# A long convolution with a gated MLP, forward and backward: two kinds of tile turned by transposing DMAs instead of TensorE

## The chip, the cores and the metric

The program runs on one core of one Trainium2 chip. The metric is device time in microseconds (us). The kernel before took 745.42 us, the median of three runs from 744.89 to 746.04. A core has TensorE (PE, with its weight loads PEld), VectorE (DVE), ScalarE (ACT), GpSimd (POOL) and SyncE (SP). SP computes nothing here: it only issues DMAs, in the order of the program, and waits on semaphores in between. ACT and POOL issue some DMAs too.

## The reference

One input `x` of 2048 x 512 in bfloat16 is normalised over its rows and goes two ways; their product is added to `x`. All gradients but that of the unused input are wanted beside the output.

```python
def _A_ref(u, ...):                      # per channel d: a kernel of length L=2048, N=128 states
    P = exp((dt * A)[:, :, None] * l)    # A, B, C complex, 512 x 128
    K = einsum("dn,dnl,dn->dl", C, P, dt * B).real
    y = irfft(rfft(pad(u.T)) * rfft(pad(K)))[:, :L].T      # long convolution
    return y + u * Dskip
def _B_ref(x, w1, w2):                   # w1: 512 x 1792, w2: 1792 x 512
    return einsum("bsf,fd->bsd", silu(einsum("bsd,df->bsf", x, w1)), w2)
...
xn = _layernorm(x)
out = x + _A_ref(xn, ...) * silu(_B_ref(xn, w1, w2))
...
_out, _vjp = jax.vjp(f, u, A_re, A_im, B_re, B_im, C_re, C_im, log_dt, Dskip, w1, w2)
return (_out, *_vjp(grad_out))
```

## The kernel before, in words

Six stages follow one another; the engines overlap across their borders. The order on every engine is the order in which the code writes the instructions (a manual schedule). A tile has a fixed number of buffers; an instruction that takes a buffer again waits for its last reader. `later` puts a call on a list and `settle` carries the list out, so that a copy out of PSUM or a store is written behind other work; a call put on the list twice over (`later` of a `later`) comes one settle later.

Stage 1 (`stage_1`) does three things beside one another, in steps that Python counts as ticks:

- The forward MLP (`gen_ffn_fwd`). The 2048 rows go in four groups `tc_` of 512, the 1792 hidden columns in seven pairs of 128-column blocks (`f0` = 0, 2, ... 12): 28 steps. A step computes `ps_h` (L607, 8 products, two PSUM buffers); ACT reads it twice, as `aT` = silu (L609) and as `hs` (L610, four buffers, shared with `o2` of the second product); SP stores `hs` to DRAM as `hTd` (L611). The second product `ps_o` (L580) of the group before goes on in the same step, and its results are stored as `gd` and `od`.
- In each step `trans` (L556 to L564) turns the `aT` pair of the step before, 128 x 1024: eight PE transposes against an identity matrix into PSUM (`pt_a`, L561), a DVE copy into `ak` (two buffers), and SP's store to `akd` in DRAM, for a later stage's gradient of `w2`.
- The tables of the Fourier transform (`dft_table_phases`). Sixteen tables `tf` of 128 x 1024 are made by DVE and ACT (or mirrored by PE, `tb_m`); four buffers. In `C(t)` (L412) SP stores one to `TFd`, eight PE transposes (L417) turn it into PSUM, and `EV` copies it to `tb_i` (two buffers), in turn by DVE (L83) and by ACT (L85). `S(t)`, one tick later, stores `tb_i` to `TId` (L423). They come in 16 of the steps from the eighth on.
- The powers of the state matrix (`power_phases`), mostly DVE and ACT, stored to `XYd` (L510), two stores at a time. Stage 2 loads `TFd` and `XYd` again.

A step ends with one settle; in the step f0 = 10 of the first three groups there is one settle more inside it.

The stages 2 to 5 form the spectra, the convolution and its gradients, the gradient of `w2` and those of the state parameters. Stage 6 (`stage_6`) has 28 steps `B.dh(n)`: SP loads `hsb` from `hTd`, three steps ahead; ACT forms `sd` (L132); PE computes `ps_da` (L1870); DVE multiplies both into `dhT` (L1871); SP stores `dhd`. Seven transposing DMAs, issued by SP after the first seven steps, bring `W1T` from DRAM (L1950), which `ps_dx` (L1893) reads, beginning after the eighth `dh`. Sixteen further transposing DMAs load `dhc` for `ps_w` (L1981), the gradient of `w1`, in 16 groups of 16 products; ACT copies each to `o10b` (three buffers), SP stores it. Between these the first output is put together (`Out0`): eight pairs of 128-row tiles, the first four by POOL's queue (`pool=True`), the last four by ACT's (`q`, L1365): a store, and three loads of the tile pair two further on.

```python
q = k.nc.gpsimd if pool else k.nc.scalar
q.dma_start(k.o0_v[:, t0:t0 + TS, :], S[:])
self.load(t0 + 2 * TS, q)
```

Of the kernel before, what the change touches and what calls it, by code (L numbers as in the profile page):

```python
# [11 lines left out]
BF16 = mybir.dt.bfloat16  # L12
I32 = mybir.dt.int32
AX = mybir.AxisListType
P = 128
# [51 lines left out]
def later(k, fn, *a, **kw):  # L67

    k.after.append((fn, a, kw))
# [303 lines left out]
def dft_table_phases(k, pool):  # L373

    nc = k.nc
    kv = pool.tile([P, 512], I32, name="kv", tag="tb_r")
    nc.gpsimd.iota(kv[:], pattern=[[4, 512]], base=1, channel_multiplier=0)
    kf = pool.tile([P, 512], F32, name="kf")
    nc.vector.tensor_copy(out=kf[:], in_=kv[:])
    lf = pool.tile([P, T], F32, name="lf")  # L380
    nc.vector.tensor_scalar(out=lf[:], in0=k.lvf[:], scalar1=1.0 / 8192.0, scalar2=None, op0=ALU.mult)
    nJ = pool.tile([P, P], BF16, name="nJ")
    nc.gpsimd.memset(nJ[:], 0.0)
    nc.gpsimd.affine_select(out=nJ[:], in_=nJ[:], compare_op=ALU.not_equal, fill=-1.0, base=1 - P, pattern=[[1, P]], channel_multiplier=1)
    st = {}

    def A(t):
        r = pool.tile([P, 512], I32, name="tb_r", tag="tb_r")
        v = pool.tile([P, 512], F32, name="tb_v", tag="tb_v", bufs=2)
        frac(nc, v[:], r[:], kf[:], lf[:, t:t + 1])  # L390
        st[t] = v

    def B(t):
        v = st[t]
        w = pool.tile([P, 512], F32, name="tb_w", tag="tb_w", bufs=2)
        nc.scalar.activation(out=w[:], in_=v[:], func=ACT.Abs)
        tf = pool.tile([P, 4, 2, P], BF16, name="tb_f", tag="tb_f", bufs=4)
        rr = lambda ap: ap.rearrange("p (a b) -> p a b", b=P)
        nc.scalar.activation(out=tf[:, :, 1, :], in_=rr(v[:]), func=ACT.Sin, scale=-2.0 * math.pi)
        nc.scalar.activation(out=tf[:, :, 0, :], in_=rr(w[:]), func=ACT.Sin, scale=-2.0 * math.pi, bias=k.halfpi[:])  # L400
        st[t] = tf

    def M(t):

        tf, tm = st[t], pool.tile([P, 4, 2, P], BF16, name="tb_m", tag="tb_f", bufs=4)
        ps = k.pd.tile([P, 2, 4, P], F32, name="ps_m", tag="pd")
        for c in range(2):
            nc.tensor.matmul(out=ps[:, c], lhsT=nJ[:], rhs=tf[:, :, 1 - c, :], start=True, stop=True)
        later(k, nc.scalar.copy, out=tm[:].rearrange("p a c b -> p c a b"), in_=ps[:])
        st[16 - t] = tm  # L410

    def C(t):  # L412
        tf = st[t]
        nc.sync.dma_start(k.TFd[:, :, t].rearrange("a p c b -> p a c b"), tf[:])
        pt = k.ps.tile([P, 8, P], BF16, name="pt_ti", tag="pz", bufs=1)
        for i in range(8):
            nc.tensor.transpose(out=pt[:, i, :], in_=tf[:, i // 2, i % 2, :], identity=k.ident[:])  # L417
        ti = pool.tile([P, 8, P], BF16, name="tb_i", tag="tb_i", bufs=2)
        later(k, EV, k, ti[:], pt[:])
        st[t] = ti  # L420

    def S(t):
        nc.sync.dma_start(k.TId[:, t], st.pop(t)[:])  # L423
    return A, B, M, C, S


# [115 lines left out]
def gen_ffn_fwd(k, fs, W1, W2):  # L542

    nc = k.nc

    def xnt(tc_):
        XNT = fs.tile([P, DK, 4, P], BF16, name="XNT", tag="XNT")
        for h in range(2):
            pt = k.ps.tile([P, 2, 4, P], BF16, name="pt_x", tag="ps")
            for d_ in range(2):  # L550
                for t in range(4):
                    dk = 2 * h + d_
                    nc.tensor.transpose(out=pt[:, d_, t, :], in_=k.xn[:, 4 * tc_ + t, dk * P:(dk + 1) * P], identity=k.ident[:])
            (nc.scalar.copy if h else nc.vector.tensor_copy)(out=XNT[:, 2 * h:2 * h + 2], in_=pt[:])
        return XNT

    def trans(tc_, aT, f0):
        pt = k.ps.tile([P, 2, 4, P], BF16, name="pt_a", tag="ps")
        for j in range(2):
            for t in range(4):  # L560
                nc.tensor.transpose(out=pt[:, j, t, :], in_=aT[:, f0 + j, t * P:(t + 1) * P], identity=k.ident[:])  # L561
        ak = fs.tile([P, 2, 4, P], BF16, name="ak", tag="ak")
        later(k, nc.vector.tensor_copy, out=ak[:], in_=pt[:])
        later(k, nc.sync.dma_start, k.akd[f0:f0 + 2, :, 4 * tc_:4 * tc_ + 4].rearrange("f p t q -> p f t q"), ak[:])  # L564

    def gen_o(tc_, aT):
        for th in range(2):
            ts_ = slice(4 * tc_ + 2 * th, 4 * tc_ + 2 * th + 2)
            g2 = fs.tile([P, 2, D], BF16, name="g2", tag="g2")
            o2 = fs.tile([P, 2, D], BF16, name="o2", tag="hs", bufs=4)  # L570
            if tc_ == 3:
                G2 = G4[:, 2 * th:2 * th + 2]
            else:
                G2 = fs.tile([P, 2, D], BF16, name="G2", tag="G2", bufs=1)[:]
                nc.sync.dma_start(G2, k.g_v[:, ts_, :])
            for t in range(2):
                tt = 2 * th + t
                pso = k.ps.tile([P, D], F32, name="ps_o", tag="ps")
                for ft in range(FT):
                    nc.tensor.matmul(out=pso[:], lhsT=aT[:, ft, tt * P:(tt + 1) * P], rhs=W2[:, ft, :], start=(ft == 0), stop=(ft == FT - 1))  # L580
                    if ft == FT // 2 - 1:
                        yield
                later(k, nc.scalar.activation, out=g2[:, t, :], in_=pso[:], func=ACT.Silu)
                later(k, nc.scalar.copy, out=o2[:, t, :], in_=pso[:])
                if t == 0:
                    yield
            later(k, nc.sync.dma_start, k.tl(k.gd[:])[:, ts_, :], g2[:])
            later(k, nc.sync.dma_start, k.tl(k.od[:])[:, ts_, :], o2[:])
            later(k, later, k, nc.vector.tensor_tensor, out=k.DS[:, ts_, :], in0=G2, in1=g2[:], op=ALU.mult)
            yield  # L590

    prev = iter(())
    XNT = xnt(0)
    late = G4 = None
    for tc_ in range(4):
        if tc_ == 3:
            G4 = fs.tile([P, 4, D], BF16, name="G4", tag="XNT")
            nc.sync.dma_start(G4[:], k.g_v[:, 12:16, :])
        aT = fs.tile([P, FT, 512], BF16, name="aT", tag="aT")
        nxt = None  # L600
        for f0 in range(0, FT, 2):
            yield
            ps = k.pd.tile([P, 2, 512], F32, name="ps_h", tag="pd")
            for j in range(2):
                ft = f0 + j
                for dk in range(DK):
                    nc.tensor.matmul(out=ps[:, j], lhsT=W1[:, dk, ft * P:(ft + 1) * P], rhs=XNT[:, dk], start=(dk == 0), stop=(dk == DK - 1))  # L607
            hs = fs.tile([P, 2, 512], BF16, name="hs", tag="hs", bufs=4)
            nc.scalar.activation(out=aT[:, f0:f0 + 2, :], in_=ps[:], func=ACT.Silu)  # L609
            nc.scalar.copy(out=hs[:], in_=ps[:])  # L610
            nc.sync.dma_start(k.hTd[tc_][:, f0:f0 + 2], hs[:])  # L611
            next(prev, None)
            if f0 == FT - 2:
                next(prev, None)
            k.mid()
            if late:
                trans(*late)
            late = (tc_, aT, f0)
            if f0 == FT - 4 and tc_ < 3:
                settle(k)  # L620
                nxt = xnt(tc_ + 1)
        XNT = nxt
        prev = gen_o(tc_, aT)
    yield
    trans(*late)
    k.last_aT = aT
    for _ in prev:
        k.mid()
        yield
# [714 lines left out]
class Out0:  # L1344
# [15 lines left out]
    def run(self, t0, pool=False):  # L1360
        k, (S, g, x) = self.k, self.ins.pop(t0)
        TT = k.nc.vector.tensor_tensor
        TT(out=S[:], in0=S[:], in1=g[:], op=ALU.mult)
        TT(out=S[:], in0=S[:], in1=x[:], op=ALU.add)
        q = k.nc.gpsimd if pool else k.nc.scalar  # L1365
        q.dma_start(k.o0_v[:, t0:t0 + TS, :], S[:])
        self.load(t0 + 2 * TS, q)

# [555 lines left out]
def stage_6(k):  # L1924
    nc = k.nc
    lo, ro = k.left, k.right
    fw = k.fw
    W1T = k.tfp.tile([P, FT, D], BF16, name="W1T", tag="W1")
# [17 lines left out]
        nc.sync.dma_start_transpose(ch[i][:, 4 * tc_:4 * tc_ + 4, :], k.dhd[tc_, FC * i:FC * i + FC])  # L1946
    for n in range(28):
        B.dh(n)
        if n < 7:
            nc.sync.dma_start_transpose(W1T[:, 2 * n:2 * n + 2], k.ins["w1"][:, 256 * n:256 * n + 256])  # L1950
        next(prev, None)
        if n == 8 or n >= 21:
            next(fin, None)
# [19 lines left out]
    for i in range(4):  # L1973
        for dk in range(DK):
# [4 lines left out]
            ps = k.ps.tile([P, FC], F32, name="ps_w1", tag="ps")  # L1979
# [49 lines left out]
```

## Time and profile before

| | |
|---|---|
| median of three runs | 745.42 us (744.89 to 746.04) |
| the profiled execution, whole | 748.97 us |
| its span, first to last instruction | 747.2 us |
| PE busy | 659.1 us, 88% |
| DVE busy | 619.4 us, 83% |
| ACT busy | 418.1 us, 56% |
| POOL busy | 122.4 us, 16% |
| DMA | 198.83 MB, mean 266 GB/s |
| mean granted TensorE clock | 0.957 of full |

The profile is of one execution; its durations belong to that one. In a line of the groups view stand: the line of the kernel, the engine, the operation, what it writes and reads, its shape, how often it ran, busy us and mean ns, and the idle time of the engine just before, with what ended it. In the waits view: who waited, for whom, us in total, how often, the longest. In the view of one tile or line: how often an instruction ran, its duration in ns as smallest, median and largest, the start of the first and the last. In the timeline: start and duration in us. "SPq" is SP's queue; its durations are those of issuing a DMA, not of the transfer. "To landing" is the time from a DMA's issue to the landing of its data. In the windows view each engine's busy us stand for a stretch of the span, then the granted clock, the mean busy share of the core's 16 DMA engines, and their GB/s. That share counts packets whose times overlap and can pass 1.

### The profile page before, as it was taken

To read this page: it belongs to the slowest core of one execution; us is meant where nothing else is said; L and a number is where in the kernel's file an instruction comes from. 1 tells how busy PE (TensorE), PEld (TensorE's weight loads), DVE (VectorE), ACT (ScalarE), POOL (GpSimd) and SP (SyncE) were. 2 spreads that over 40 slices of the span, in tenths; PEclk is the share of its full clock that TensorE was granted. 3 is DMA by queue.
4 is the path that set the end of the run, shared out by engine and by line. 5 is a ranking of instruction groups with operands and counts; after the bars stand their busy time and mean duration, and the time that the engine had idled before them with its cause. 6 is when DMAs were issued, how large, how long until landed. Compare 5 with 4: busy or idle time off the path is not lost. (4 is left out here: it accounts for less than half of the span.)

```text
span 747.2 us, 13309 instructions
## 1 busy us (share of the span) xinstructions
PE 659.1 (88%) x5132; PEld 336.8 (45%) x5132; DVE 619.4 (83%) x965; ACT 418.1 (56%) x513; POOL 122.4 (16%) x184
## 2 busy tenths in 40 slices
PE   4778877799878777999999899999999979999988
PEld 2434444354545656554444344444444434444543
DVE  6799999989899799599999999944577549899570
ACT  4789888995568967365534322344656523443231
POOL 2334171021011002100001212041222002200000
PEclk9998998899999998999999999999999989999999
DMA  9647767889898978999767879799886997999992
GB/s 268 236 165 246 236 229 240 266 298 358 268 317 275 301 222 182 296 347 359 287 227 286 287 288 353 215 316 335 272 283 232 240 307 248 321 242 221 225 266 87
DMA packets 167361, 198.83 MB, mean 266 GB/s; under 512 B 58461, under 2 KB 128484, under 8 KB 161378
## 3 DMA queue, kind: packets, MB, share of 16 engines
q1 hardware_dynamic: 150882, 132.63, 58.1%
q0 software_dynamic: 11200, 51.98, 19.8%
q10 hardware_dynamic: 5216, 13.38, 5.4%
q8 instruction: 40, 0.66, 0.4%
q14 instruction: 23, 0.19, 0.1%
HBM read 105.38 MB, written 83.38 MB: 253 GB/s over the span
## 5 line engine op out<-in xcount | busy, mean ns | idle before, releaser
L607 PE MATMUL ps_h<-XNT,W 128*128 128x512 bf16 x224 | 60.8, 421 | 12.2 <-ACT hs L610 12.2
L1188 PEld LDWEIGHTS <-TIs 128*128 128x128 bf16 x384 | 37.7, 99 | 51.7 <-issue 4.9
L1893 PE MATMUL ps_dx<-W1T,dhT 128*128 128x512 bf16 x224 | 53.8, 384 | 5.5 <-DMA W1T<-in_B_w_dram 4.6
L580 PE MATMUL ps_o<-W,aT 128*128 128x512 bf16 x224 | 55.7, 399 | 2.5 <-DVE ak L76 2.5
L1870 PE MATMUL ps_da<-DOT,W2T 128*128 128x512 bf16 x224 | 53.9, 388 | 2.3 <-DVE dhT L1871 2.3
L1981 PE MATMUL ps_w<-dhc,xn 128*128 128x448 bf16 x256 | 51.3, 361 | 3.1 <-ACT o10b L1983 3.1
L1595 PE MATMUL ps_w<-DO_all,AW 128*128 128x512 bf16 x224 | 52.0, 380 | 0.0
L1871 DVE TENSOR_TENSOR dhT<-ps_da,sd 128x1024 bf16<-128x1024 f32 x28 | 34.1, 1222 | 18.9 <-ACT sd L132 14.0
L1902 ACT ACTIVATE dxn<-dxn,c,rstd 128x512 f32<-128x512 f32 x16 | 13.0, 814 | 65.6 <-DVE c L1901 65.6
L1781 DVE TENSOR_TENSOR T<-Vb,YTl 128x2048 bf16<-128x2048 bf16 x16 | 19.6, 1224 | 35.2 <-ACT Vb L1772 34.9
L1164 PEld LDWEIGHTS <-TFs 128*128 128x128 bf16 x312 | 30.1, 98 | 38.6 <-issue 2.1
L934 ACT COPY XT<-pt_xt 128x1024 bf16<-128x1024 bf16 (+1 forms) x44 | 41.4, 1009 | 5.2 <-DMA XTd<-XT 3.2
L1772 ACT CAST Vb<-ps_V 128x1024 bf16<-128x1024 f32 x32 | 31.7, 1013 | 16.8 <-PE ps_V L1770 11.5
L1164 PE MATMUL ps_f<-K_b,TFs 128*128 128x512 bf16 x168 | 39.1, 379 | 1.5 <-DMA K_b<-Kud 1.3
L607 PEld LDWEIGHTS <-W 128*128 128x128 bf16 x224 | 22.8, 106 | 38.3 <-issue 21.8
L1981 PEld LDWEIGHTS <-xn 128*128 128x128 bf16 x256 | 25.5, 100 | 28.1 <-issue 5.6
L580 PEld LDWEIGHTS <-aT 128*128 128x128 bf16 x224 | 22.9, 102 | 32.0 <-issue 8.3
L1893 PEld LDWEIGHTS <-dhT 128*128 128x128 bf16 x224 | 22.0, 99 | 33.3 <-issue 7.5
L1870 PEld LDWEIGHTS <-W2T 128*128 128x128 bf16 x224 | 22.0, 99 | 30.2 <-issue 6.4
L998 PE MATMUL ps_f<-xn,TFs 128*128 128x512 bf16 x128 | 32.7, 411 | 3.3 <-DMA TFs<-TFd 3.3
L1164 PE MATMUL ps_f<-DS,TFs 128*128 128x512 bf16 x144 | 33.0, 379 | 1.8 <-ACT S_s L1443 1.8
L932 PE MATMUL pt_xt<-ident_bfloat,X 128*128 128x128 bf16 x328 | 25.7, 228 | 8.9 <-ACT XT L934 6.9
(342 smaller groups left out, 1510.6 us busy)
## 6 DMA issues: line engine op xcount, KB each, us to landing
TIs<-TId SPq DMA_DIRECT2D x24, 512.0 KB, 6.6
XTd<-XT SPq DMA_DIRECT2D x20, 512.0 KB, 5.8
XTl<-XTd SPq DMA_DIRECT2D x15, 512.0 KB, 8.6
hTd<-hs SPq DMA_DIRECT2D x28, 256.0 KB, 3.5
akd<-ak SPq DMA_DIRECT2D x28, 256.0 KB, 3.3
UXl<-UXd POOLq DMA_DIRECT2D x7, 1024.0 KB, 7.7
dhd<-dhT SPq DMA_DIRECT2D x28, 256.0 KB, 4.2
XYd<-XYg SPq DMA_DIRECT2D x25, 256.0 KB, 4.0
```

The costliest lines, as they stand in the source:

```text
L580: nc.tensor.matmul(out=pso[:], lhsT=aT[:, ft, tt * P:(tt + 1) * P], rhs=W2[:, ft, :], start=(ft == 0), stop=(ft == FT - 1))
L607: nc.tensor.matmul(out=ps[:, j], lhsT=W1[:, dk, ft * P:(ft + 1) * P], rhs=XNT[:, dk], start=(dk == 0), stop=(dk == DK - 1))
L934: nc.scalar.copy(out=XT[:, j0:j0 + len(ks)], in_=pt[:, 0:len(ks)])
L998: nc.tensor.matmul(out=ps[:, c, :], lhsT=TFs[:, t1 + 4 * j, c, :], rhs=src[:, t1 + 4 * j, :], start=(j == 0), stop=(j == 3))
L1164: nc.tensor.matmul(out=ps[:, c, :], lhsT=tab(j), rhs=at(t1 + 4 * j), start=(n == 0), stop=(n == 4 * len(terms) - 1))
L1188: nc.tensor.matmul(out=ps[:, j, :], lhsT=TIs[:, j, 2 * kt + c, :], rhs=B[kt][:, c, (t0 + j) % 4, :], start=(kt == 0 and c == 0), stop=(kt ...
L1595: nc.tensor.matmul(out=ps[:], lhsT=A[:, t, :], rhs=k.DO[:, t, :], start=(t == 0), stop=(t == T - 1))
L1772: nc.scalar.copy(out=self.V[i][:, g2], in_=ps[:].rearrange("p b c n -> p c b n"))
L1870: nc.tensor.matmul(out=ps[:, j], lhsT=self.W2T[:, ft // 2, dk, j * P:(j + 1) * P], rhs=self.DOT[tc_][:, dk], start=(dk == 0), stop=(dk == ...
L1871: nc.vector.tensor_tensor(out=self.dhT[:, f0:f0 + 2, :], in0=ps[:], in1=sd[:], op=ALU.mult)
L1893: nc.tensor.matmul(out=psx[:], lhsT=dhT[:, ft, t % 4 * P:(t % 4 + 1) * P], rhs=self.W1T[:, ft, :], start=(ft == 0), stop=(ft == FT - 1))
L1981: nc.tensor.matmul(out=ps[:], lhsT=k.xn[:, t, dk * P:(dk + 1) * P], rhs=ch[i][:, t, :], start=(t == 0), stop=(t == T - 1))
```

## The change

- `C(t)`: the eight PE transposes, their PSUM tile and the copy by DVE or ACT go. SP issues one transposing DMA from the table in SBUF to `tb_i` in SBUF. 16 times.
- `trans`: likewise, one transposing DMA from `aT` to `ak`; the store to `akd` is put off by one settle more, since it now waits for a DMA. 28 times.
- `W1T`: the seven transposing DMAs are issued after the first four steps of stage 6, two after each (one after the fourth), instead of one after each of the first seven.
- `Out0.run`: the last four tile pairs are stored, and their followers loaded, by SP's queue instead of ACT's.

```diff
     def C(t):
         tf = st[t]
         nc.sync.dma_start(k.TFd[:, :, t].rearrange("a p c b -> p a c b"), tf[:])
-        pt = k.ps.tile([P, 8, P], BF16, name="pt_ti", tag="pz", bufs=1)
-        for i in range(8):
-            nc.tensor.transpose(out=pt[:, i, :], in_=tf[:, i // 2, i % 2, :], identity=k.ident[:])
         ti = pool.tile([P, 8, P], BF16, name="tb_i", tag="tb_i", bufs=2)
-        later(k, EV, k, ti[:], pt[:])
+        nc.sync.dma_start_transpose(ti[:], tf[:].rearrange("p a c b -> p (a c b)"))
         st[t] = ti
...
     def trans(tc_, aT, f0):
-        pt = k.ps.tile([P, 2, 4, P], BF16, name="pt_a", tag="ps")
-        for j in range(2):
-            for t in range(4):
-                nc.tensor.transpose(out=pt[:, j, t, :], in_=aT[:, f0 + j, t * P:(t + 1) * P], identity=k.ident[:])
         ak = fs.tile([P, 2, 4, P], BF16, name="ak", tag="ak")
-        later(k, nc.vector.tensor_copy, out=ak[:], in_=pt[:])
-        later(k, nc.sync.dma_start, k.akd[f0:f0 + 2, :, 4 * tc_:4 * tc_ + 4].rearrange("f p t q -> p f t q"), ak[:])
+        nc.sync.dma_start_transpose(ak[:].rearrange("p j t q -> p (j t) q"), aT[:, f0:f0 + 2, :].rearrange("p j t -> p (j t)"))
+        later(k, later, k, nc.sync.dma_start, k.akd[f0:f0 + 2, :, 4 * tc_:4 * tc_ + 4].rearrange("f p t q -> p f t q"), ak[:])
...
-        q = k.nc.gpsimd if pool else k.nc.scalar
+        q = k.nc.gpsimd if pool else k.nc.sync
         q.dma_start(k.o0_v[:, t0:t0 + TS, :], S[:])
...
-        if n < 7:
-            nc.sync.dma_start_transpose(W1T[:, 2 * n:2 * n + 2], k.ins["w1"][:, 256 * n:256 * n + 256])
+        for m in range(2 * n, min(2 * n + 2, 7)):
+            nc.sync.dma_start_transpose(W1T[:, 2 * m:2 * m + 2], k.ins["w1"][:, 256 * m:256 * m + 256])
```

## The prediction

> **What bounds the kernel now.** I read the windows first, then the groups of lines, the waits of SP's queue, single tiles and the timeline. The chain of work that ended last cannot be followed back before 392 us, so the first stage, in which nearly all of the change lies, is read from its own windows. Its 28 steps store one `hTd` each, and I take 17 to 181 us as the stretch around them.
>
> ```profile
> core 0: us, PE busy (x) PEld busy (x) DVE busy (x) ACT busy (x) POOL busy (x), PEclk, DMA share, GB/s
> 17.00:181.00 164.00, 137.51 (x877) 72.35 (x876) 154.54 (x312) 139.28 (x175) 44.06 (x36) 0.91 0.73 251
> 45.00:166.00 121.00, 98.74 (x632) 52.18 (x631) 116.31 (x223) 108.32 (x136) 34.45 (x28) 0.89 0.74 249
> ```
>
> From 45 to 166 us DVE is busy 116.3 of 121 us (96%), ACT 90%, PE 82%, and the DMA engines 74%. DVE is the bound there, with ACT close behind. SP is not in this table. Its queue waits in the stretch like this (the longest and the shortest of 21 rows, which sum to 94.9 us), and its stores mark the steps:
>
> ```profile
> SPq L611 <- ACT hs L610: 58.8, 24, 5.9
> ...
> SPq L76 <- DMA akd<-ak: 0.2, 1, 0.2
> ...
> L611 SPq DMA_DIRECT2D hTd<-hs x28: 319/320/581, 17.9 to 166.2; - x28
> ...
> 44.71 0.32 SPq L611 DMA_DIRECT2D hTd<-hs  x1
> 97.86 0.32 SPq L611 DMA_DIRECT2D hTd<-hs  x1
> 108.56 0.32 SPq L611 DMA_DIRECT2D hTd<-hs  x1
> ```
>
> So SP waits 94.9 us, 58.8 of them for ACT's `hs`, and issues for about 164 - 94.9 = 69.1 us. SP is in order: one wait holds back everything behind it. That slack is what the change spends. The store at 44.71 is the eighth of the 28: the seven steps up to it take 3.8 us each, the twenty after it 121.5 / 20 = 6.1 us; the longest is 10.7 us, from 97.86 to 108.56.
>
> **The change, part by part.** First what leaves the compute engines:
>
> ```profile
> L76 DVE COPY ak<-pt_a 128x1024 bf16<-128x1024 bf16 x28 | 19.1, 683 | 3.7 <-DMA akd<-ak 3.4
> L83 DVE COPY tb_i<-pt_ti 128x1024 bf16<-128x1024 bf16 x8 | 5.4, 680 | 1.5 <-DMA XYd<-XYg 1.5
> L85 ACT COPY tb_i<-pt_ti 128x1024 bf16<-128x1024 bf16 x8 | 8.5, 1059 | 0.0
> L561 PE MATMUL pt_a<-ident_bfloat,aT 128*128 128x128 bf16 x224 | 17.6, 224 | 0.5 <-DVE ak L76 0.5
> L417 PE MATMUL pt_ti<-ident_bfloat,tb_f 128*128 128x128 bf16 x72 | 5.6, 222 | 0.9 <-DVE tb_i L83 0.9
> L417 PE MATMUL pt_ti<-ident_bfloat,tb_m 128*128 128x128 bf16 x56 | 4.3, 219 | 0.0
> ```
>
> DVE loses 19.1 + 5.4 = 24.5 us, ACT 8.5, PE 27.5. In the stretch that leaves DVE 154.5 - 24.5 = 130.0, ACT 139.3 - 8.5 = 130.8, PE 110. With DVE's present idle time (164 - 154.5 = 9.5) on top, the engines alone could do the stretch in about 140 us: 24 us less, the most that this can bring.
>
> In their place SP issues 28 transposes of `ak` and 16 of `tb_i`, each 128 x 1024 bf16, 256 KB, from SBUF to SBUF. No such transfer is in the trace. The nearest is W1T's, also 256 KB, but out of DRAM; then `dhc`'s, 448 KB:
>
> ```profile
> L1950 SPq DMA_TRANSPOSE W1T<-in_B_w_dram x7: 1363/1452/1600, 581.7 to 597.7; - x7
> DMA to landing us min/median/max: 4.7/5.2/5.8
> ...
> L1946 SPq DMA_TRANSPOSE dhc<-dhd x16: 1537/1930/3315, 662.8 to 713.1; - x16
> ```
>
> A transpose occupies SP for 1.45 us and lands 5.2 us after its issue. Stores of that size are quicker:
>
> ```profile
> akd<-ak SPq DMA_DIRECT2D x28, 256.0 KB, 3.3
> ...
> 69.25 0.32 SPq L611 DMA_DIRECT2D hTd<-hs  x1
> 70.46 0.44 SPq L414 DMA_DIRECT2D TFd<-tb_f  x1
> 71.01 0.51 SPq L76 DMA_DIRECT2D akd<-ak  x1
> 71.56 1.09 SPq L510 DMA_DIRECT2D XYd<-XYg  x2
> 72.75 0.66 SPq L423 DMA_DIRECT2D TId<-tb_i  x1
> ```
>
> SP's new account, in five terms:
> (a) Issues: 44 x 1.45 = 63.8 us. Ends: 44 x 0.32 = 14 (`hTd`'s store) and 44 x 3.3 = 146 (the longest `dhc`). I take W1T's median, same size and same kind.
> (b) The store `TId` now waits on SP for its own transpose to land. In program order the transposes of `tb_i` and `ak`, an `akd` store and sometimes two `XYd` stores stand before it: 1.45 + 1.45 + 0.45 = 3.35, or 4.4 with 1.09 more. It lands at 5.2, so SP stands still 0.8 to 1.85, say 1.3, 16 times: 21 us. What is queued behind is the next `hTd`, whose `hs` has four buffers: engines can run two to three steps ahead, no more. At a landing of 3.3 the term is nothing, at 5.8 about 30.
> (c) At the three early settles (step f0 = 10 of the first three groups), `akd` stands one store behind its own transpose: 5.2 - 1.45 - 0.4 = 3.35, three times: 10 us; 5 at a landing of 3.3, 12 at 5.8.
> (d) `ak` has two buffers, and a buffer is held from the transpose's issue to the landing of its store: 5.2 + 0.4 + 3.3 = 8.9 per two steps, 4.4 a step. The first seven steps take 3.8 us now; 0.6 us more in each is 4 us; nothing at a landing of 3.3, 7 at 5.8. Later steps have room.
> (e) SP cannot work ahead of ACT, so a step that DVE makes long leaves SP idle. In the one of 10.7 us SP would have 0.32 + 0.44 + 1.45 + 1.45 + 0.51 + 1.09 + 0.66 = 5.9 us to do: 4.8 idle, of which I let half be filled by what it is behind with: 2.4; ends 0 and 4.8.
> Sum: 69.1 + 63.8 + 21 + 10 + 4 + 2.4 = 170.3 us, 6.3 more than the 164 of the stretch. SP becomes the bound, just. DVE's 24.5 us turn into DVE waiting for buffers.
>
> The DMA engines say nearly the same. Transposes go in small packets; here are the 16 us from 700 to 716 with hardly anything else, and then the rate in W1T's stretch (584 to 600 us):
>
> ```profile
> DMA packets 12515, 3.67 MB, mean 229 GB/s; under 512 B 11747, under 2 KB 12515, under 8 KB 12515
> q1 hardware_dynamic: 12515, 3.67, 110.7%
> ...
> q1 hardware_dynamic: 8389, 4.60, 113.1%
> ```
>
> 1.107 x 16 us x 16 engines / 12515 = 22.6 ns a packet. Without its 768 larger packets of about 1 KB the window leaves 2.9 MB in 11,747 packets, 249 B each, so I count 256 B: 256 KB are 1,024 packets, 1.45 us of all 16 engines; 44 are 64 us. The stretch has 0.73 x 164 = 120 us now, so 184 us, and at the highest share that I find held (113%) 163 us: as long as the stretch. Other end: at a copy's price (251 GB/s at 0.73 is 344 GB/s, 0.76 us each) it is (120 + 33) / 1.13 = 136 us. I keep 1.45, the price of the same kind. [...]
>
> W1T's, two a step instead of one:
>
> ```profile
> 588.42 0.54 SPq L1856 DMA_DIRECT2D hsb<-hTd  x1
> 593.16 1.06 ACT L132 ACTIVATE sd<-hsb 128x1024 bf16<-128x1024 bf16 x1 [1.63 <-DMA hsb<-hTd]
> 597.67 1.45 SPq L1950 DMA_TRANSPOSE W1T<-in_B_w_dram  x1
> 603.28 1.01 PE L1893 MATMUL ps_dx<-W1T,dhT 128*128 128x512 bf16 x2 [3.44 <-DMA W1T<-in_B_w_dram]
> ```
>
> SP issues without a gap here, so its order decides. The seventh transpose moves from 597.7 to about 593.6 and lands near 599, and PE's 3.4 us wait at 603.3 goes. But the `hsb` loads between are pushed back by the transposes ahead of them, that of 588.4 to 592.6. ACT already waits for it, so `sd` slips from 593.2 to about 597 and PE's next `ps_da` with it to about 599; the remaining seven `ps_dx` then end near 603.5 instead of 604.3. Net -0.8 us; ends -3.4 (PE's whole wait) and +4.2 (the load's whole delay).
>
> Out0's last four tiles: ten issues (four stores, six loads) leave ACT for SP.
>
> ```profile
> 720.27 13.95 PE L1981 MATMUL ps_w<-dhc,xn 128*128 128x448 bf16 x64 [2.69 <-ACT o10b L1983]
> 734.30 9.25 PE L1981 MATMUL ps_w<-dhc,xn 128*128 128x448 bf16 x48
> ```
>
> From 720.3 us PE runs to the end without an idle moment over 0.2 us, so ACT's freed issues bring nothing. What could cost: an `o10b` store stands behind four issues of 0.4 us, 1.6 us later. `o10b` has three buffers and 16 products of `ps_w` take 3.03 us (48 in 9.25), so it is needed 9 us later: 0, at most +1.6. PE's run is the cover; without it the 1.6 would be paid.
>
> Sum: 6.3 - 0.8 + 0 = +5.5. The profiled execution took 748.97 us (span 747.2), so the changed one would take 754.5; the median of the three runs shown is 745.42, 3.6 lower, so I forecast 745.42 + 5.5 = 750.9.
>
> **The rivals.** First, faster: a transpose that never leaves SBUF issues in W1T's shortest 1.36 us and lands like a store, at 3.3. SP then needs 69 + 60 + 5 + 2 = 136 us and is not the bound; engines (140) and DMA (between 136 and 163, middle 150) are. A stretch of 154, which leaves 4 us for steps that do not match, gives -10 and with W1T's -0.8 734.6. For it: SP's 94.9 us of waiting; against: each of W1T's took 4.7 us or more to land. It decides where the landing is under about 4 us.
>
> The second rival rests on one row more:
>
> ```profile
> 667.26 2.45 SPq L1946 DMA_TRANSPOSE dhc<-dhd  x1
> ```
>
> Second, far slower: a transpose out of SBUF holds SP longer than one out of DRAM. At 2.45 us, which `dhc`'s second issue took behind loads and stores (667.26 us), SP needs 69 + 108 + 10 + 4 + 2, with nothing for (b): 193, +29, and with W1T's -0.8 774. Each 0.1 us of hold is 4.4 us. For it: `dhc`'s spread up to 3.3 us while other transfers are queued, as they are here. [...] No row here shows a transpose out of SBUF.
>
> Third, no change: SP's excess is taken up after the last step, when PE still has the last output products to do and SP little, or the engines run the two to three steps ahead that `hs` allows; only W1T's -0.8 is left, 744.6.
>
> **How the numbers follow.** Forecast (SP and DMA just over the stretch, +1.5 to +18) 0.47; faster 0.30; far slower 0.15; no change 0.08. A measurement of this kernel tells about 0.2%, 1.5 us, from no change. So slower 0.62, same 0.08, faster 0.30. The range 736 to 772 holds the forecast and no change whole, some two thirds of the faster case and a third of the far slower one, 0.8 together. The likeliest case's own range is 747 to 763.
>
> **What would show it.** In the changed kernel's first stage: a transpose of `ak` at 1.4 to 1.6 us on SP and 5 us to landing; SP waiting 40 us or less instead of 94.9, and for DMA landings instead of `hs`; DVE under 85% busy from 45 us to the stage's end with waits for DMA; a DMA share near 1.0. The last `hTd` comes at 166 us or later. W1T's wait of 3.4 us is gone and the waits for `hsb` are longer. The end from 720 us keeps its shape. I am wrong if SP still waits 40 us or more for `hs` (then DVE or ACT still set the pace and the time falls), or if a transpose holds SP for 2 us or more.

## The result, and the profile after

| | before | after |
|---|---|---|
| median of four runs | 745.15 us (744.15 to 746.04) | 776.30 us (775.25 to 783.44) |
| span of the profiled execution | 747.2 us | 773.6 us |
| mean granted TensorE clock | 0.957 | 0.938 |
| DMA, whole span | 198.83 MB | 210.32 MB |

The ratio is 1.044 with a 95% interval from 1.037 to 1.050: the kernel became 31 us slower, where 5.5 us were forecast and 772 was the upper end. The sign was right; the time lies outside the range. Ratios, here and below, are estimated from the executions in the chip's faster state alone, while the medians are of all, so a ratio is not the quotient of two medians. The two profiled executions differ by 26.4 us of span (that of before lay 3.6 us above the median it was shown with, that of after 0.9 below its own).

The windows of the changed kernel, with the columns named in the first line:

```profile
core 0: us, PE busy (x) PEld busy (x) DVE busy (x) ACT busy (x) POOL busy (x), PEclk, DMA share, GB/s
17.00:181.00 164.00, 116.55 (x514) 50.44 (x512) 117.87 (x261) 127.04 (x160) 36.81 (x34) 0.84 1.04 279
45.00:166.00 121.00, 79.83 (x333) 33.87 (x333) 84.48 (x174) 92.25 (x117) 24.12 (x22) 0.80 1.05 285
181.00:215.00 34.00, 11.60 (x32) 4.12 (x32) 14.71 (x19) 8.79 (x11) 4.88 (x8) 0.70 0.97 247
```

DVE, the bound before at 96%, is busy for 84.5 of 121 us (70%), ACT for 92.3 (76%), PE for 79.8 (66%). No compute engine sets the pace any more. The DMA share went from 0.74 to 1.05, but the rate only from 249 to 285 GB/s.

SP's queue in the 164 us (the first three and the last of 19 rows of its waits, which sum to 25.3 us instead of 94.9), then single tiles and lines of the changed kernel:

```profile
SPq L556 <- DMA akd<-ak: 6.4, 5, 2.4
SPq L76 <- DMA ak<-aT: 4.7, 4, 1.3
SPq L604 <- ACT hs L603: 4.7, 3, 2.4
...
SPq L76 <- ACT b_s L501: 0.2, 1, 0.2
```

```profile
L556 SPq DMA_TRANSPOSE ak<-aT x28: 1232/1552/3703, 20.3 to 201.9; - x28
L76 SPq DMA_DIRECT2D akd<-ak x28: 360/577/1362, 27.6 to 205.7; - x28
...
L416 SPq DMA_TRANSPOSE tb_i<-tb_f x9: 1399/1677/1745, 45.8 to 172.8; - x9
L416 SPq DMA_TRANSPOSE tb_i<-tb_m x7: 1412/1565/1761, 62.9 to 165.1; - x7
...
L604 SPq DMA_DIRECT2D hTd<-hs x28: 320/502/1372, 18.1 to 183.3; - x28
...
ak<-aT SPq DMA_TRANSPOSE x26, 3.6
tb_i<-tb_f SPq DMA_TRANSPOSE x9, 4.2
tb_i<-tb_m SPq DMA_TRANSPOSE x7, 4.6
```

A transpose out of SBUF holds SP for 1.55 to 1.68 us; by the last three rows (the issues from 17 to 181 us, median us to landing) it lands after 3.6 to 4.6. The wait for `hs`, 58.8 us before, is down to 4.7. Plain issues take longer: an `hTd` store 0.50 us instead of 0.32. The last `hTd` leaves at 183.3 us instead of 166.2, 17.1 us later. Two more marks, of before and of after, tell where the other 9 us come from:

```profile
L639 SPq DMA_DIRECT2D TFs<-TFd x5: 332/373/744, 180.9 to 313.5; - x5
```

```profile
L632 SPq DMA_DIRECT2D TFs<-TFd x5: 332/347/706, 210.2 to 339.7; - x5
...
L1943 SPq DMA_TRANSPOSE W1T<-in_B_w_dram x7: 1288/1411/1572, 608.5 to 620.7; - x7
```

SP's first load of `TFs`, at the border to stage 2, comes 29.3 us later (210.2 against 180.9), W1T's first transpose 26.8 (608.5 against 581.7), the end 26.4. So the loss has two places: 17.1 us in the 28 steps and 12.2 at the border behind them. The stages between return 2.5, and stage 6 is about even.

What happens at the border, in the timeline of SP's queue, then of DVE and of PE, and in the windows of the changed kernel:

```profile
179.86 2.16 SPq L556 DMA_TRANSPOSE ak<-aT  x1
182.07 1.17 SPq L76 DMA_DIRECT2D akd<-ak  x1
183.29 1.09 SPq L604 DMA_DIRECT2D hTd<-hs  x1
197.78 1.23 SPq L556 DMA_TRANSPOSE ak<-aT  x1
```

```profile
192.22 1.09 DVE L812 TENSOR_TENSOR m<-X 128x1792 bf16<-128x1792 bf16 x1 [8.32 <-DMA X<-XYd]
...
197.63 2.74 PE L991 MATMUL ps_f<-xn,TFs 128*128 128x512 bf16 x6 [16.64 <-DMA TFs<-TFd]
```

```profile
184.00:188.00 4.00, 0.00 (x0) 0.00 (x0) 0.00 (x0) 0.00 (x0) 0.00 (x0) 0.75 1.27 140
188.00:192.00 4.00, 0.00 (x0) 0.00 (x0) 0.00 (x0) 0.00 (x0) 0.00 (x0) 0.50 0.99 109
```

From 184 to 192 us no compute engine does anything. SP stands for 13.4 us before the last transpose of `ak` but one (issued at 197.78), until the `akd` store issued at 182.07 has landed and given its buffer back. PE waits 16.6 us for `TFs`, DVE 8.3 for `X`. POOL's queue had issued these loads, 2.5 MB with `XYc`, between 178.7 and 182.8 us, just as SP issued a transpose and two stores. That transpose, of 179.86, took 13.3 us to land (view of the DMA issues from 181 to 184 us), where those before it took 3.6 in the median:

```profile
TFs<-TFd POOLq DMA_DIRECT2D x1, 1024.0 KB, 15.4
...
ak<-aT SPq DMA_TRANSPOSE x1, 13.3
```

The DMA engines show a full share in those 8 us and move only 109 to 140 GB/s.

### The profile page after: what moved, and what is told of

It is laid out like the page before. It is cut to its first block, busy times and chain, and to the rows that moved or that the text cites. A ratio compares the mean times of both kernels' runs of the same rounds, so it can differ in the third digit from the quotient of the medians.

```text
span 773.6 us, 12573 instructions
## 1 busy us (share of the span) xinstructions
PE 640.3 (83%) x4780; PEld 313.5 (41%) x4780; DVE 592.6 (77%) x929; ACT 410.6 (53%) x505; POOL 117.0 (15%) x184
## 2 busy tenths in 40 slices
DMA packets 213822, 210.32 MB, mean 272 GB/s; under 512 B 104925, under 2 KB 174948, under 8 KB 207842
## 5 line engine op out<-in xcount | busy, mean ns | idle before, releaser
L600 PE MATMUL ps_h<-XNT,W 128*128 128x512 bf16 x224 | 63.3, 434 | 30.7 <-ACT hs L603 27.4
L991 PE MATMUL ps_f<-xn,TFs 128*128 128x512 bf16 x128 | 36.3, 444 | 25.8 <-DMA TFs<-TFd 23.5
L1157 PEld LDWEIGHTS <-TFs 128*128 128x128 bf16 x312 | 30.2, 98 | 38.3 <-issue 3.7
L991 PEld LDWEIGHTS <-TFs 128*128 128x128 bf16 x160 | 17.1, 111 | 49.3 <-DMA TFs<-TFd 24.4
L132 ACT ACTIVATE sd<-hsb 128x1024 bf16<-128x1024 bf16 x28 | 28.7, 1047 | 14.0 <-DMA hsb<-hTd 13.6
```

The costliest lines, as they stand in the source:

```text
L132: nc.scalar.activation(out=out, in_=in_, func=ACT.Derivative_silu)
L991: nc.tensor.matmul(out=ps[:, c, :], lhsT=TFs[:, t1 + 4 * j, c, :], rhs=src[:, t1 + 4 * j, :], start=(j == 0), stop=(j == 3))
L1157: nc.tensor.matmul(out=ps[:, c, :], lhsT=tab(j), rhs=at(t1 + 4 * j), start=(n == 0), stop=(n == 4 * len(terms) - 1))
```

## The experiments

Three theories stand in the expectations. **Q**: SP's queue is the bound, as the prediction had it first. **D**: the 16 DMA engines are; with this mix they move about 285 GB/s and no more. **L**: at the border transposes and POOL's large loads are in flight together, and both become slow. Beside them stands the simplest one, that the parts add up.

### Each part alone

All four begin from the kernel before, which took 747.8 us on that chip.

```diff
 C(t), e1 alone:
-        ... eight nc.tensor.transpose into pt_ti; later(k, EV, k, ti[:], pt[:])
+        nc.sync.dma_start_transpose(ti[:], tf[:].rearrange("p a c b -> p (a c b)"))
 trans, e2 alone:
-        ... eight nc.tensor.transpose into pt_a; later(k, nc.vector.tensor_copy, out=ak[:], in_=pt[:])
+        nc.sync.dma_start_transpose(ak[:]..., aT[:, f0:f0 + 2, :]...)
-        later(k, nc.sync.dma_start, k.akd[...]..., ak[:])
+        later(k, later, k, nc.sync.dma_start, k.akd[...]..., ak[:])
 stage 6, e3 alone:
-        if n < 7:
+        for m in range(2 * n, min(2 * n + 2, 7)):
 Out0.run, e4 alone:
-        q = k.nc.gpsimd if pool else k.nc.scalar
+        q = k.nc.gpsimd if pool else k.nc.sync
```

> Kernel before, with only the sixteen transform tables turned by DMA. Theory Q (SP's queue is the bound in the changed kernel: 44 issues of 1.55 to 1.7 us, and every other issue longer): SP would issue for about 69 + 16 x 1.6 + some 10 = 105 of 164 us, no bound, so the 5.4 us of DVE and 8.5 us of ACT come through in part: 2 to 6 us faster. Theory D (the 16 DMA engines are the bound, share 1.05 through the whole stage): 120 + 16 x 1.45 = 143 of 164, no bound either, the same 2 to 6 us faster. Theory L (transposes that meet POOL's large loads at the end of stage 1 make both slow): the last table is turned well before the end, so no loss. A slower time than before would speak against all three and for a cost per step of the landing.

> Kernel before, with only the 28 activation pairs turned by DMA. Q: SP issues 69 + 28 x 1.5 + 10 = 121 of 164 us, no bound; DVE loses 19 us, so 5 to 12 us faster, less whatever the end costs. D: 120 + 28 x 1.45 = 161 DMA-engine us in 164, at the edge: 0 to 5 us faster. L: the last two or three transposes still meet POOL's loads of the next stage, so 8 to 13 us of stall there, seen as a transpose of ak waiting for its store: 0 to 8 us slower in all.

> Kernel before, with only W1T's transposes two a step. The prediction's term: -0.8 us (from -3.4 to +4.2); PE's 3.4 us wait for W1T gone, waits of ACT for hsb longer by some us.

> Kernel before, with only the first output's last tiles on SP's queue. The prediction's term: 0 (at most +1.6 us); PE's run from about 720 us to the end keeps its length.

| part alone | median | ratio, 95% interval |
|---|---|---|
| tables by DMA | 745.1 | 0.999 (0.996 to 1.002) |
| `ak` by DMA | 752.9 | 1.005 (1.001 to 1.009) |
| W1T two a step | 744.9 | 0.997 (0.995 to 1.000) |
| Out0 by SP | 748.8 | 1.004 (1.001 to 1.006) |

The ratios come to -0.8 + 3.9 - 1.9 + 2.7 = +3.9 us together; the whole change cost 31. So the parts do not add up: something that each has room for alone is used up by the two kinds of transposes together. For the tables all three theories gave a gain of 2 to 6 us; the ratio gives 0.8, and its interval reaches from 3 us faster to 1.3 slower, so no gain is shown. For `ak`, Q and D gave a gain and missed; only L had a loss of up to 8 us in its band. With `ak` alone the last `hTd` even came earlier, at 164.4 us; its loss is at the border. Its waits of SP and POOL's load of `TFs` (the profiled execution took 763.4 us, 10.5 above this kernel's median, so its rows may show more of this wait than most executions have):

```profile
SPq L559 <- DMA akd<-ak: 30.7, 11, 18.4
...
TFs<-TFd POOLq DMA_DIRECT2D x1, 1024.0 KB, 20.8
```

Out0 by SP, in PE's timeline at the end of the kernel: the small product ahead of the last run, and that run, of the kernel before, of e4, and of the changed kernel:

```profile
734.15 0.22 PE L985 MATMUL pt_row<-ident_bfloat,ob 128*4 128x128 bf16 x1
```

```profile
729.82 0.22 PE L985 MATMUL pt_row<-ident_bfloat,ob 128*4 128x128 bf16 x1 [1.75 <-ACT o10b L1983]
730.31 9.24 PE L1981 MATMUL ps_w<-dhc,xn 128*128 128x448 bf16 x48 [0.27 <-ACT o10b L1983]
```

```profile
760.22 0.22 PE L978 MATMUL pt_row<-ident_bfloat,ob 128*4 128x128 bf16 x1 [1.38 <-ACT o10b L1976]
760.98 9.24 PE L1974 MATMUL ps_w<-dhc,xn 128*128 128x448 bf16 x48 [0.55 <-ACT o10b L1976]
```

PE waits here for a copy that waits for its `o10b` buffer, whose store now shares SP's queue with Out0's ten issues: 2.0 us in e4, 1.9 in the changed kernel. Both waits are also in e5, e8, e11 and e12, whose Out0 goes by SP, and are missing in the kernel before, e1, e2, e3, e9 and e10, where it goes by ACT.

### Which resource: three additions and a removal

These four begin from the changed kernel; 748.5 us was the kernel before on their chip.

```diff
 e5: the last three pairs (tc_ == 3, f0 >= 8) by PE and DVE, as before the change
+        if tc_ == 3 and f0 >= 8:
+            ... eight transposes, copy and store as in the kernel before
+            return
 e6: 28 more small DMAs on SP
             nc.sync.dma_start(k.hTd[tc_][:, f0:f0 + 2], hs[:])
+            nc.sync.dma_start(k.scr[7 * tc_ + f0 // 2:7 * tc_ + f0 // 2 + 1], k.ident[0:1, :])
 e7: 28 issues taken from SP
-            nc.sync.dma_start(k.hTd[tc_][:, f0:f0 + 2], hs[:])
+            nc.scalar.dma_start(k.hTd[tc_][:, f0:f0 + 2], hs[:])
 e8: 28 more stores of 256 KB, issued by ACT
             nc.sync.dma_start(k.hTd[tc_][:, f0:f0 + 2], hs[:])
+            nc.scalar.dma_start(k.scr[tc_][:, f0:f0 + 2], hs[:])
```

> Changed kernel, but the last three activation pairs (fourth group, f0 = 8, 10, 12) are turned by PE and DVE as before, so that no transpose is in flight when POOL issues the next stage's large loads. Theory L (the two kinds of transfer slow each other at the stage's end, and the next transpose waits for the store of two before): the 13.4 us wait of the ak transpose for its store and the idle 8 us of DVE and 16 us of PE for those loads go, 10 to 14 us faster than the changed kernel, about 764. If that wait is only backlog of the queue: 2 to 4 us faster, about 773.

> Changed kernel with one more DMA of 256 bytes per step on SP's queue, 28 in all: issue time without load on the DMA engines. Theory Q (SP's issuing is the bound): 28 x 0.4 to 0.5 = 11 to 14 us slower than the changed kernel, about 789. Theory D (the DMA engines are the bound: the changed kernel's extra 36 x 0.262 MB between the eighth and the last step at the 285 GB/s that it moved there are 33 us of engine time, of which 17 showed): 0 to 3 us, 776 to 779.

> Changed kernel with the 28 hTd stores issued by ACT, right behind the copy that makes hs, instead of by SP. The DMA engines' load is the same. Q: 28 x 0.5 = 14 us less on SP, and its waits for hs go: 8 to 14 us faster than the changed kernel, 762 to 768. D: no gain, 774 to 778. The stall at the stage's end stays in both.

> Changed kernel with every hs stored a second time, to a scratch tensor, by ACT's queue: 28 x 256 KB more for the DMA engines and no issue more on SP. D: 28 x 0.262 MB at 285 GB/s are 26 us: 795 to 802. Q: 776 to 781, what is left is ACT's 28 issues of about 0.4 us in a stage where ACT is 76% busy.

| from the changed kernel | median | ratio to before, 95% interval | last `hTd` at |
|---|---|---|---|
| unchanged | 776.3 | 1.044 (1.037 to 1.050) | 183.3 us |
| e5, last three `ak` by PE | 766.3 | 1.025 (1.017 to 1.032) | 179.9 |
| e6, 28 small DMAs more on SP | 785.0 | 1.049 (1.041 to 1.057) | 183.5 |
| e7, `hTd` issued by ACT | 780.5 | 1.044 (1.032 to 1.055) | 188.5 |
| e8, 28 x 256 KB more, not by SP | 798.3 | 1.067 (1.059 to 1.075) | 202.2 |

The rows of `hTd` in e6, e7 and e8, and e8's window:

```profile
L605 SPq DMA_DIRECT2D hTd<-hs x28: 320/492/1691, 18.6 to 183.5; - x28
```

```profile
L604 ACTq DMA_DIRECT2D hTd<-hs x28: 326/327/358, 18.0 to 188.5; - x28
```

```profile
L605 SPq DMA_DIRECT2D hTd<-hs x28: 320/442/902, 18.9 to 202.2; - x28
...
45.00:166.00 121.00, 68.01 (x283) 28.90 (x289) 70.74 (x124) 83.79 (x107) 24.15 (x22) 0.79 1.05 290
```

Q falls: 28 further issues on SP leave the last `hTd` where it was (183.5 us), and taking 28 issues away does not bring it forward: in e7 it came 5.2 us later (188.5), which no run explains, and the 780.5 us lie 2.5 above D's band and 12.5 above Q's. The median of e6 lies between what Q and D gave, but its interval overlaps the changed kernel's, so the row decides, not the time. D stands: 20 of e8's 28 stores fall behind the eighth step, 5.24 MB, which at its 290 GB/s is 18.1 us; the last `hTd` moved by 18.9, and the share stayed at 1.05.

L, by e5: SP's longest wait for an `akd` store, its window at the border, and POOL's load of `TFs` in e5; SP's first own load of `TFs`; then POOL's load in the kernel before (15.4 us in the changed one):

```profile
SPq L566 <- DMA akd<-ak: 5.9, 5, 1.7
...
185.00:193.00 8.00, 6.28 (x16) 2.30 (x16) 6.75 (x24) 0.11 (x1) 0.00 (x0) 0.57 1.03 399
...
TFs<-TFd POOLq DMA_DIRECT2D x1, 1024.0 KB, 12.1
...
L642 SPq DMA_DIRECT2D TFs<-TFd x5: 332/348/462, 200.4 to 329.6; - x5
```

```profile
TFs<-TFd POOLq DMA_DIRECT2D x1, 1024.0 KB, 11.9
```

Without a transpose beside POOL's loads the same DMA engines move 399 GB/s, the load is as quick as before, and the wait of 13.4 us is gone. Three transposes fewer, out of 44, win 10 us by the medians and 14 by the ratios (the two kernels ran on two chips). Only the first of the three had met POOL's loads; the other two were issued after the wait. SP's first `TFs` load comes 9.8 us sooner (200.4 against 210.2), 3.4 of them by the last `hTd`. So e5 takes back 6.4 of the 12.2 us lost at the border; the other 5.8 stay, and no run tells why. That the slow 8 us come of transposes and POOL's loads together is shown; why the engines serve them so slowly is not. Nor is the stall always as long: in e6, e7 and e8, which keep all 44 transposes, SP's longest wait for `akd` is 11.2, 8.9 and 7.4 us, and in e7 POOL's load of `TFs` takes 13.1.

### Doses, bytes and a better kernel

e9 is the kernel before with the first and third part; e10 is e2 with its last three pairs by PE; e11 is the changed kernel with f0 = 0, 4, 8, 12 by PE; e12 is the changed kernel with plain DMAs in place of the transposing ones.

```diff
 e10:
+        if tc_ == 3 and f0 >= 8:
+            ... as in the kernel before
 e11:
+        if f0 % 4 == 0:
+            ... as in the kernel before
 e12:
-        nc.sync.dma_start_transpose(ti[:], tf[:].rearrange("p a c b -> p (a c b)"))
+        nc.sync.dma_start(ti[:].rearrange("p i b -> p (i b)"), tf[:].rearrange("p a c b -> p (a c b)"))
...
-        nc.sync.dma_start_transpose(ak[:]..., aT[:, f0:f0 + 2, :]...)
+        nc.sync.dma_start(ak[:].rearrange("p j t q -> p (j t q)"), aT[:, f0:f0 + 2, :].rearrange("p j t -> p (j t)"))
```

> The kernel before with two of the four parts of the change: the tables turned by DMA and W1T's transposes two a step. `ak` stays with PE and DVE, Out0 with ACT's queue. Alone the two gave ratios of 0.9989 and 0.9974 to the kernel before. They lie 400 us apart and share no buffer, so if the cost of the whole change is the two kinds of transposes together (theory D: about 285 GB/s is all that the 16 DMA engines move with this mix; the tables alone need 34.3 MB from 45 to 166 us, a share of 0.96), the two gains add up: ratio 0.994 to 0.998, 741.5 to 744 us for 745.2. If the tables' DMAs only put the loss off to a later stage: 0.999 or more.

> The kernel before with `ak` turned by DMA, but for the last three of the 28 pairs, which PE and DVE turn as before; the tables stay with PE. With all 28 by DMA the ratio was 1.0052, though the last `hTd` came 1.8 us earlier than before; an `akd` landing late (18.4 us) and POOL's load of TFs (20.8 us to landing against 11.9) stood behind it. Theory L (transposes in flight beside POOL's large loads at the stage's end make both slow): the wait for `akd` falls under 5 us, TFs lands within 14 us, and the ratio is 0.993 to 1.000. Theory D by itself (too many bytes for the DMA engines, wherever they lie): three transposes fewer are 0.8 MB or 2.8 us at 285 GB/s at the most, and those not on the path: 1.002 to 1.006.

> The changed kernel with 16 of the 28 `ak` pairs (f0 = 0, 4, 8, 12) back with PE and DVE: 12 `ak` transposes instead of 28, the 16 of the tables stay. Theory D as a dose: from the eighth step's `hTd` on about 30.1 + 25 x 0.262 = 36.7 MB are to be moved, at 285 GB/s 129 us, so the last `hTd` comes near 174 us, between 166.2 (before) and 183.3 (all 28); the DMA share from 45 to 166 us stays at 1.00 to 1.05. With the half of the wait at the stage's end gone too the time is 752 to 763 us (ratio 1.009 to 1.024). If not the bytes but a queue or buffer shared by the two kinds were the matter, the first few transposes would do it and the last `hTd` would stay at 180 or more, ratio over 1.035.

> The changed kernel with its 44 transposing DMAs of the first stage replaced by plain DMAs of the same 256 KB between the same tiles, with the same waits and the same stores behind them. It leaves the turning out (`TId` and `akd` hold unturned tiles), so its output is not the reference's; the number and order of all instructions are the same. Theory D in its exact form (a transpose costs the DMA engines 1,024 packets of 256 bytes, some 24 ns each; the same bytes in packets of 2 KB cost half of that or less): the DMA share from 45 to 166 us falls to 0.95 or less, the last `hTd` comes at 150 to 168 us, no `akd` wait of 13 us is left at the stage's end, time 732 to 748 us. If the bytes or the number of DMAs and waits were the cost and not the small packets: the last `hTd` stays at 178 or later, time 768 to 780 us. SP's hold tells a third thing: if the plain DMAs hold SP for 0.4 us instead of 1.55 the account of SP falls by 44 x 1.1 = 50 us too, so this run alone does not part SP from the DMA engines; the runs with more issues and more bytes did that.

| | median (before on that chip) | ratio, 95% interval | last `hTd` at |
|---|---|---|---|
| e9, tables by DMA and W1T two a step | 746.3 (745.9) | 1.001 (0.998 to 1.004) | 166.1 us |
| e10, `ak` by DMA but the last three | 749.2 (745.9) | 1.003 (0.999 to 1.007) | 160.8 |
| e11, 12 `ak` and 16 tables by DMA | 760.4 (745.9) | 1.021 (1.015 to 1.026) | 172.5 |
| e12, all 44 as plain copies | 748.9 (746.3) | 1.002 (0.999 to 1.006) | 158.2 |

e9 missed the sum of the two gains (0.994 to 0.998): they do not come back when the parts are joined. Alone their intervals reached to 1.002 and 1.000, so neither gain was shown; that the tables put a loss off to a later stage is not excluded (0.999 or more was given for that). And I have no version that beats the kernel before.

e10 bears out L by its rows: SP's longest wait for `akd` is 2.3 us instead of 18.4, and `TFs` lands within 11.6. But its ratio, 1.0029, lies in the band that D had by itself (1.002 to 1.006), and its interval touches L's (0.993 to 1.000) only with its lower end, 0.9992. In time, L is shown by e5 only. That wait, and e10's window:

```profile
SPq L569 <- DMA akd<-ak: 11.3, 8, 2.3
...
45.00:166.00 121.00, 90.53 (x498) 44.23 (x498) 103.05 (x207) 105.62 (x134) 32.75 (x27) 0.87 1.03 299
```

The window adds why the two kinds do not go together: with `ak`'s transposes alone the DMA share is already 1.03, though the steps still end at 160.8 us. The tables' transposes come on top of that.

e11 gives the dose. Forecast were a last `hTd` near 174, a share of 1.00 to 1.05 and 752 to 763 us; all three came. The row and the window:

```profile
L614 SPq DMA_DIRECT2D hTd<-hs x28: 319/384/668, 18.2 to 172.5; - x28
...
45.00:166.00 121.00, 83.28 (x427) 38.60 (x425) 102.98 (x195) 97.93 (x125) 28.70 (x22) 0.87 1.00 281
```

e12 leaves the turning out: `TId` and `akd` hold unturned tiles. So it separates the bytes from the turning. First the DMA view of e12 from 45 to 166 us, rows of its single lines (the hold of `ak`'s DMA, the marks of `hTd` and `XYd`) and its window; then the DMA view of the changed kernel; then that of the kernel before, with its mark of `XYd`:

```profile
DMA packets 29753, 40.05 MB, mean 331 GB/s; under 512 B 2399, under 2 KB 15199, under 8 KB 29738
...
L556 SPq DMA_DIRECT2D ak<-aT x28: 470/554/721, 20.2 to 171.7; - x28
...
L604 SPq DMA_DIRECT2D hTd<-hs x28: 319/414/1065, 18.0 to 158.2; - x28
...
L507 SPq DMA_DIRECT2D XYd<-XYg x25: 438/595/1473, 44.4 to 175.8; - x25
...
45.00:166.00 121.00, 90.89 (x393) 39.08 (x392) 103.97 (x210) 100.33 (x129) 33.28 (x27) 0.87 0.96 331
```

```profile
DMA packets 55026, 34.44 MB, mean 285 GB/s; under 512 B 34851, under 2 KB 46371, under 8 KB 55020
```

```profile
DMA packets 25004, 30.09 MB, mean 249 GB/s; under 512 B 1808, under 2 KB 15120, under 8 KB 24993
...
L510 SPq DMA_DIRECT2D XYd<-XYg x25: 319/534/1979, 49.2 to 173.4; - x25
```

The same bytes between the same tiles, behind the same waits, move at 331 GB/s instead of 285, at a share of 0.96 (0.95 or less was expected), and the 28 steps end 25 us sooner (158.2 against 183.3). So neither the bytes nor the waits cost the time, but the turning, which makes 33,000 packets under 512 bytes. Whether the size of these packets or the turning itself sets their price stays open: no run moves the tiles unturned in packets of that size. The run does not part SP's shorter hold (0.55 us instead of 1.55) from the packets either; e6, e7 and e8 do that.

e12 missed the band of 732 to 748 us, though: its steps end 8 us before those of the kernel before, and its time does not fall. It still has Out0 on SP, which alone measured +2.7 us. SP's `TFs` load comes at 179.8, only 1.1 us earlier than before. The last store of `XYd`, by the chain of the powers, which stage 2's loads need, is at 175.8 us here and was at 173.4. That this store holds the border is my reading of these rows; no run moved it by itself.

## Why the prediction was wrong

**The step that failed is the DMA engines' term**: "at the highest share that I find held (113%) 163 us: as long as the stretch". Its price of 1.45 us a transpose was about right. In the changed kernel's window from 45 to 166 us there are 34,851 - 1,808 = 33,043 more small packets, 32.3 transposes of 1,024. At 256 B each, the prediction's estimate, they hold 8.5 MB; the other 26.0 MB at the price of before (0.74 x 121 us for 30.09 MB) take 77.3 us of all engines, the whole 1.05 x 121 = 127, so 49.7 us are left for 32.3, an estimate of 1.54 us each. The share was the error. 113% came from 16 us of W1T's stretch, six transposes beside 13 plain transfers of 256 KB; over 121 us it was 1.05, in the changed kernel and in e8 alike, and none of e1, e2 and e5 to e12 shows more from 45 to 166 us. With both numbers (120 + 44 x 1.54) / 1.05 = 179 us, +15 instead of -1; measured were +17.1. (By the last `hTd` 42 of the 44 had been issued; with these it is 176, +12.) The term of the sum should have been this one. SP's account, which I made the bound "just", came out near the same size by chance, 170 against 163, and hid it. The forecast had the sign right by that account, which did not hold: that is luck.

**SP's account.** (a) held: 1.55 and 1.57 to 1.68 us an issue for 1.45, 44 of them some 70 us for 63.8. (b) was 21 us and measured 2.2 (1.1 each behind tables from `tb_f` and `tb_m`): the transposes land at 3.6 to 4.6, not 5.2, and the issues in between are longer. (c) was 10; all of SP's waits for `ak` sum to 4.7. (d) was 4 and the waits for `akd` sum to 6.4. SP stands still for 25.3 us in all and is not the bound, as e6 and e7 show. "SP waiting 40 us or less, and for DMA landings instead of `hs`" and "DVE under 85%" came true, and still do not prove the cause that I had put behind them: a DMA share of 1.05 came with the same signs.

**The border after the last step** was missing from the sum. I costed the transposes up to the last `hTd` and did not ask what else is in flight there. It is 12.2 us of the 26.4.

**W1T**, -0.8: PE's waits for it are gone, ACT's for `hsb` grew from 6.8 to 13.6 us over the stage, as the step said. Alone it measured 0.997 with an interval that touches 1.000, and in e9 nothing: the sign is open.

**Out0**, 0 and at most +1.6: measured alone +2.7 us (1.001 to 1.006). The cover that I named, PE's run without idle time, does not hold: PE now waits 1.9 to 2.0 us for `o10b` just ahead of its last run, where it did not wait before. I counted four issues ahead of one store; ten go through the same queue, and each store that is late holds one of three buffers.

**The rivals.** The far slower one gave 774, close to the measured 776.3, but by another mechanism: it needs a hold of 2.45 us, and 1.55 was measured. The faster one was said to decide under a landing of about 4 us; the transposes land at 3.6 to 4.6, about there, and the kernel is slower, since that rival had the DMA engines at 136 to 163 us by the same 113%. Its 136 us were worked out at a copy's price, which tiles turned within SBUF did not have: from 45 to 166 us e12 with plain copies moves 331 GB/s and the changed kernel 285, and a plain copy holds SP for 0.55 us, a transpose for 1.55. "No change" fell with the rest.

## What to carry to other kernels

Before work goes from compute engines to DMA, add up the DMA engines' time for the whole stretch, with the price of turned tiles (here an estimated 1.54 us of all 16 engines for 256 KB, twice the 0.76 estimated for a plain copy from 251 GB/s at a share of 0.73), and divide by a share that a long stretch held (here 1.05 over 121 us), not by the highest of a short one (1.13 over 16). An edit that looks free alone is no evidence for two of them: here each kind of transpose cost at most some 4 us on its own, and the whole change 31. Look also at what else is in flight when the moved transfers end: taking three of 44 transposes back won 10 us, most of it where one of them had met the next stage's loads.

## What the runs showed of the hardware

- Transposes and POOL's loads in flight together: a full DMA share at 109 and 140 GB/s for 8 us, and 399 GB/s in the same place without the transposes (e5). POOL's load of `TFs`, 1 MB, took 15.4 us in the changed kernel, 13.1 in e7 and 20.8 in e2 instead of the 11.9 of before, and a transpose of `ak` in the changed kernel 13.3 us to land.
- The store of `hTd` held SP for 0.50 us in the changed kernel instead of 0.32, and ACT for 0.33 in e7, at a DMA share of 1.04 (45 to 166 us). So in e7 that share alone did not make this issue longer.
- PE's clock was low right behind the stall: granted were 0.50 from 198 to 202 us, when PE was at work again, and the 128 products of `ps_f` from `xn`, which begin there, took 444 ns each in the mean, against 411 before.
